# First two token tiles of x transposed by DMA instead of by identity matmuls, with the wq and wk loads issued from ACT's queue

## The chip, the cores and the metric

The kernel runs on one core of a Trainium2 chip. A core has TensorE (PE; its weight loads are listed as PEld), VectorE (DVE), ScalarE (ACT), GpSimd (POOL) and SyncE (SP), and 16 DMA engines that move data between the chip's memory and the core's on-chip memory. DMAs are issued here by SP, and a few by ACT, each through a hardware queue of its own. The metric is the device time of one execution in microseconds (us), as the median of several runs; lower is better.

## The reference

Two blocks read the same x (2048 tokens of 512) and a per-token gate mixes them. The heart of it:

```python
g = _sigmoid((x * gate_w).sum(-1, keepdims=True))
# A: linear attention, 32 heads of 16
q, k, v = split_heads(x @ wqkv)
pq, pk = phi(q), phi(k)             # phi(t) = where(t > 0, t + 1, exp(t)) + 1e-6
kv = einsum("bhsd,bhse->bhde", pk, v)
z = einsum("bhsd->bhd", pk)
o = einsum("bhqd,bhde->bhqe", pq, kv) / (einsum("bhqd,bhd->bhq", pq, z)[..., None] + 1e-6)
a = o @ wo
# B: gated MLP, inner width 1376
b = (_silu(x @ w1) * (x @ w3)) @ w2
return g * a + (1 - g) * b
```

All arrays are bfloat16.

## The kernel before

The 2048 tokens are 16 tiles of 128. A matmul of this chip contracts over the partitions, so x is needed in two forms: xN, with the tokens on the partitions (as it lies in memory), and xT, with the 512 features on the partitions in four k-chunks of 128.

The stages follow each other on TensorE, and the order of the instructions is written out by hand (`tc.manual_schedule()`): each engine runs its own list in program order and waits on semaphores where it needs another's result.

Stage 1, about the first 47 us, projects q and k for each tile with the weights wqk (512 rows by 1024 columns, four pieces of 128 rows, one for each k-chunk) and applies phi: ACT takes the exponential from PSUM (L182), DVE does the rest (L184, L187). `g_step` (L215) accumulates xN-transposed times phi(k) over all tiles in the banks 0 to 3 of PSUM; POOL sums phi(k) for z. Stage 2 runs, for each of four blocks of 512 tokens, the gated MLP's first half (`glu_step`, L259), and between its steps the small products that fold the attention into one matrix; then `out_step` (L423) makes each tile's output.

What concerns the change is the start:

- SP issues the loads in program order. The first is xN for the tokens 0 to 255 (L119). It lays two neighbouring tokens on each partition: partition p holds the tokens 2p and 2p+1, so "tile 0" is the even and "tile 1" the odd ones, and the output of these two tiles is written back in the same interleaved order (L451). Then come the four pieces of wqk (L116, `load_wqk`), then from L127 on the transposed loads of the tiles 2 to 15 (`load_xT`, L113, a DMA that transposes on the way) with the rest of xN between them (`natural`, L126), and then the weights of the later stages.
- ACT issues one small load, `touch` (L123): 16 columns of two k-chunks of wqkv into a tile that nothing reads.
- POOL builds a 128x128 identity matrix, `ident` (L69).
- TensorE starts with 13 matmuls on a constant (`warm_step`, L315, L331), whose result is not used. Then it transposes the tiles 0 and 1 itself: a matmul of a 128x128 block of xN with the identity (`transpose_block`, L321) puts the transposed block into PSUM, and DVE and ACT copy it into xT (L337 to L340, L352). Six of the eight blocks come first; the two of the last k-chunk come after the first four projection matmuls (L351).
- The first projections (`first_mm`, L344) go by k-chunk, as the pieces of wqk land: for the k-chunks 0 and 1 each of k and q for the tiles 0 and 1; then k alone for the chunks 2 and 3, and the two phi steps are started; then q for the chunks 2 and 3; then the k projection of tile 2 (L363). After the eight matmuls of chunk 0 and 1 the order is thus k tile 0, k tile 1 on piece 2, the same on piece 3, and ten more matmuls before the first `g_step` (L365).

The lines that set this order:

```python
for kc in range(2):
    for n, t in (("k", 0), ("q", 0), ("k", 1), ("q", 1)):
        first_mm(n, t, kc)
    ...
for kc in range(2, KC):
    for t in range(2):
        first_mm("k", t, kc)
```

Of the kernel before, what the change touches and what calls it, by code (L numbers as in the profile page):

```python
# [7 lines left out]

ACT = mybir.ActivationFunctionType
ALU = mybir.AluOpType  # L10
# [2 lines left out]
BF16 = mybir.dt.bfloat16  # L13
# [3 lines left out]
def kernel(  # L17
# [17 lines left out]
    nc = tc.nc  # L35
    P = nc.NUM_PARTITIONS

    Bb, S, D = A_x.shape
# [15 lines left out]
    x2d = A_x.flatten_outer_dims()  # L54
    out2d = out.flatten_outer_dims()
    x_t = x2d.rearrange("(t p) d -> p t d", p=P)
    wqkv_r = A_wqkv.rearrange("(kc d) n -> d kc n", d=P)
# [3 lines left out]
    consts = ctx.enter_context(tc.tile_pool(name="consts", bufs=1))  # L61
# [3 lines left out]
    ctx.enter_context(tc.manual_schedule())  # L65

    warm = nc.const_aps.tensor(1.0, [P, 256], BF16)
    ident = consts.tile([P, P], BF16, name="ident")
    make_identity(nc, ident[:])  # L69


    bmask = consts.tile([P, HPC, Dh], BF16, name="bmask")
# [2 lines left out]
        out=bmask[:], in_=bmask[:], pattern=[[-Dh, HPC], [0, Dh]], compare_op=ALU.is_ge,  # L75
# [3 lines left out]
        out=bmask[:], in_=bmask[:], pattern=[[Dh, HPC], [0, Dh]], compare_op=ALU.is_ge,  # L79
# [17 lines left out]
    xN = consts.tile([P, NT, D], BF16, name="xN")  # L97
    wqk = consts.tile([P, KC, 2 * D], BF16, name="wqk")
# [8 lines left out]
    xT = consts.tile([P, KC, S], BF16, name="xT")  # L107
    act_pre = consts.tile([P, 1], BF16, name="act_pre")
    dq = nc.sync

    def load_xT(t):
        ts = slice(t * P, (t + 1) * P)
        dq.dma_start(out=xT[:, :, ts], in_=x2d[ts, :], transpose=True)  # L113

    def load_wqk(kc):
        dq.dma_start(out=wqk[:, kc, :], in_=wqkv_r[:, kc, 0 : 2 * D])  # L116

    x_first = x2d[0 : 2 * P, :].rearrange("(p j) d -> p j d", j=2)
    dq.dma_start(out=xN[:, 0:2, :], in_=x_first)  # L119
    nc.scalar.activation(out=act_pre[:], in_=warm[:, 0:1], func=ACT.Exp)  # L120

    touch = consts.tile([P, 2, 16], BF16, name="touch")
    nc.scalar.dma_start(out=touch[:], in_=wqkv_r[:, 1:3, 0:16])  # L123
    for kc in range(KC):
        load_wqk(kc)
    natural = {3: (2, 4), 5: (4, 8), 8: (8, 16)}  # L126
    for t in range(2, NT):  # L127
        load_xT(t)
# [3 lines left out]
    with nc.allow_non_contiguous_dma(reason="gate column"):  # L132
        dq.dma_start(
            out=wr[:, :, 2 * FR : NR], in_=gate_w.rearrange("(kc d o) -> d kc o", d=P, o=1)
# [21 lines left out]
    bank = [psum.tile([P, D], FP32, name=f"bank{i}") for i in range(8)]  # L156
    turn = {"mm": 0, "ab": 0}

    def mm_tile():
        turn["mm"] += 1  # L160
        return bank[4 + (turn["mm"] - 1) % 4]

    def ab_tile():
        turn["ab"] += 1
        return bank[(turn["ab"] - 1) % 4]
# [149 lines left out]
    def warm_step(n):  # L315
        for _ in range(n):
            nc.tensor.matmul(  # L317
                bank[7][:, 0:256], lhsT=warm[:, 0:P], rhs=warm, start=True, stop=True
            )

    def transpose_block(t, kc, dst):  # L321

        nc.tensor.matmul(  # L323
            dst, lhsT=xN[:, t, kc * P : (kc + 1) * P], rhs=ident[:], start=True, stop=True
        )

    def transpose_kc(kc, ps):
        for t in range(2):
            transpose_block(t, kc, ps[:, t * P : (t + 1) * P])

    warm_step(13)  # L331

    for t in range(2):
        transpose_block(t, 0, bank[t][:, 0:P])
    transpose_kc(1, bank[2])
    transpose_kc(2, bank[3])
    nc.vector.tensor_copy(out=xT[:, 0, 0:P], in_=bank[0][:, 0:P])  # L337
    nc.scalar.activation(out=xT[:, 0, P : 2 * P], in_=bank[1][:, 0:P], func=ACT.Copy)
    nc.vector.tensor_copy(out=xT[:, 1, 0 : 2 * P], in_=bank[2][:, 0 : 2 * P])
    nc.scalar.activation(out=xT[:, 2, 0 : 2 * P], in_=bank[3][:, 0 : 2 * P], func=ACT.Copy)  # L340
    first = {(t, n): mm_tile() for n, t in (("k", 0), ("k", 1), ("q", 0), ("q", 1))}
    w_of = {"k": wk, "q": wq}

    def first_mm(n, t, kc):  # L344
        proj_mm(first[t, n], t, w_of[n], kc)

    for kc in range(2):
        for n, t in (("k", 0), ("q", 0), ("k", 1), ("q", 1)):
            first_mm(n, t, kc)
        if kc == 0:  # L350
            transpose_kc(3, bank[0])  # L351
            nc.vector.tensor_copy(out=xT[:, 3, 0 : 2 * P], in_=bank[0][:, 0 : 2 * P])  # L352
    for kc in range(2, KC):
        for t in range(2):
            first_mm("k", t, kc)
# [67 lines left out]
    def out_step(tb, tt):  # L423
        t = tb * TPB + tt
        ts = slice(t * P, (t + 1) * P)
        tl = slice(tt * P, (tt + 1) * P)
        a_ps = ab_tile()
        for c in range(KC):
            nc.tensor.matmul(  # L429
                a_ps[:], lhsT=pqT[:, c, ts], rhs=M2[:, c, :],  # L430
                start=(c == 0), stop=(c == KC - 1),
            )
        aga = work.tile([P, D], FP32, tag="aga", name="aga")
        nc.scalar.activation(out=aga[:], in_=a_ps[:], func=ACT.Copy, scale=g_all[:, t : t + 1])  # L434
        o = work.tile([P, D], BF16, tag="o", bufs=3, name="o")
        last = t == NT - 1
        for lo, w in ((0, 2 * P), (2 * P, P), (3 * P, P)) if last else ((0, D),):
            cs = slice(lo, lo + w)
            b_ps = ab_tile()
            for fc in range(FC + 1):  # L440
                n = P if fc < FC else FR
                nc.tensor.matmul(  # L442
                    b_ps[:, 0:w], lhsT=hT[tb][:n, fc, tl], rhs=w2[:n, fc, cs],
                    start=(fc == 0), stop=(fc == FC),
                )
            nc.vector.scalar_tensor_tensor(  # L446
                out=o[:, cs], in0=b_ps[:, 0:w], scalar=omg_all[:, t : t + 1], in1=aga[:, cs],
                op0=ALU.mult, op1=ALU.add,
            )
            if t < 2:  # L450
                rows = out2d[0 : 2 * P, :].rearrange("(p j) d -> p j d", j=2)[:, t, :]  # L451
            else:
                rows = out2d[ts, :]
            if last and w == P:

                if lo + w < D:
                    continue
                cs = slice(2 * P, D)
            dq.dma_start(out=rows[:, cs], in_=o[:, cs])
# [3 lines left out]
    for tb in range(NTB):  # L463
        for fc in range(FC):
            glu_step(tb, fc)
            if tb == 0:
                if fc in den_at:
                    den_step(den_at[fc])
                if fc == 2:
                    kv_step()  # L470
                if fc == 4:
                    m2_step()
                    z_order()
                    den_products(0)
                if fc == 7:
                    rem_step(0)
        for tt in range(TPB):
            out_step(tb, tt)
            if tb + 1 < NTB:
                if tt == 0:  # L480
                    hT[tb + 1] = work.tile([P, FC + 1, TB], BF16, tag="hT", name="hT")
                if tt == 1:
                    rem_step(tb + 1)
                den_step((tb + 1) * TPB + tt)
# [30 lines left out]
```

## Time and profile before

| What | Value |
|---|---|
| Time, median of 3 runs (lowest to highest) | 179.23 us (178.83 to 179.74) |
| Span of the profiled execution, first to last instruction | 177.9 us |
| TensorE busy | 174.3 us, 98% |
| DVE, ACT, POOL busy | 101.5, 62.2, 63.5 us |
| First DMA issue (SP, L119), first matmul (L317) | 0.81, 0.84 us |
| First transposing matmul (L323), first projection (L169) | 3.74, 4.51 us |
| First g_step matmul (L217) | 9.76 us |

For the profiled execution the page gives the span and no time of its own; the median of the runs lies 1.3 us above that span and the lowest run 0.9 us. TensorE's matmuls are pipelined: the profile's length of one matmul (0.38 us for 128x512) is longer than the distance from one to the next, so the pace is read from the chain, as the length of a piece divided by its count. "Landing" of a DMA is the time from its issue to the moment its completion is told.

### The profile page before, as it was taken

The numbers are of one execution on the slowest core, as the hardware profiler recorded it, in microseconds if no ns is written. First come the engines' busy times: TensorE is split into PE (matmuls) and PEld (weight loads), VectorE is DVE, ScalarE is ACT, GpSimd is POOL, SyncE is SP. The second block draws the span as 40 slices with busy tenths as digits, with TensorE's granted clock in tenths as the row PEclk, the third lists the DMA queues.
The fourth block names the chain that finished last, engine by engine and source line by source line (L and its number), as shares of the span: only waits on it lengthen the run. The fifth ranks groups of instructions, "written<-read, shape, count | busy, mean of one in ns | idle before, by whom it ended". The sixth has DMA issues, their size and how long they took to land.

```text
span 177.9 us, 2504 instructions
## 1 busy us (share of the span) xinstructions
PE 174.3 (98%) x879; PEld 84.1 (47%) x879; DVE 101.5 (57%) x195; ACT 62.2 (35%) x113; POOL 63.5 (36%) x105
## 2 busy tenths in 40 slices
PE   8999999999999999999999999999999999999993
PEld 5444444444454464644444464444445444444453
DVE  0299798888865888666344166634325564333222
ACT  3255444544744332331333223242321223342130
POOL 5077667557301676846300044540004432000000
DMA  6978959993103025243100013520000342000001
GB/s 175 266 209 233 168 100 315 391 350 111 33 0 29 0 55 66 66 95 106 29 0 4 0 33 85 94 57 4 0 0 29 88 92 59 0 0 0 29 33 59
DMA packets 29724, 15.41 MB, mean 87 GB/s; under 512 B 21552, under 2 KB 28048, under 8 KB 29712
## 3 DMA queue, kind: packets, MB, share of 16 engines
q1 hardware_dynamic: 29440, 15.25, 35.2%
q8 instruction: 7, 0.11, 0.3%
q10 hardware_dynamic: 272, 0.01, 0.1%
q14 instruction: 5, 0.04, 0.1%
HBM read 8.56 MB, written 2.10 MB: 60 GB/s over the span
## 4 chain that ended last, share of the span: by engine, by line
PE 98%; DVE 0%; issue 0%
PE bank L442 21%; PE bank L264 19%; PE bank L270 19%; PE bank L169 16%; PE bank L429 8%; PE bank L217 8%; PE bank L231 3%; PE bank L317 2%; PE bank L323 1%; PE bank L404 1%; PE bank L417 0%; DVE o L446 0%
## 5 line engine op out<-in xcount | busy, mean ns | idle before, releaser
L276 DVE TENSOR_TENSOR hT<-bank,sg 128x512 bf16<-128x512 f32 x40 | 27.3, 682 | 32.4 <-PE bank L270 32.4
L264 PE MATMUL bank<-xT,w 128*128 128x512 bf16 x160 | 41.1, 379 | 0.0
L270 PE MATMUL bank<-xT,w 128*128 128x512 bf16 x160 | 41.1, 379 | 0.0
L442 PE MATMUL bank<-w,hT 128*128 128x512 bf16 (+3 forms) x198 | 40.7, 355 | 0.0
L275 ACT ACTIVATE sg<-bank 128x512 bf16<-128x512 f32 x40 | 23.9, 597 | 46.7 <-PE bank L264 46.7
L298 POOL TENSOR_TENSOR pqs<-pq,rden 128x512 bf16<-128x512 bf16 x16 | 16.9, 1056 | 55.7 <-issue 48.2
L169 PE MATMUL bank<-wqk,xT 128*128 128x512 bf16 x128 | 31.2, 386 | 0.0
L442 PEld LDWEIGHTS <-hT 128*128 128x128 bf16 (+1 forms) x198 | 18.5, 98 | 19.8
L446 DVE SCALAR_TENSOR_TENSOR o<-bank,omg_all,aga 128x512 bf16<-128x512 f32 (+2 forms) x18 | 12.4, 692 | 25.6 <-PE bank L442 25.5
L201 POOL TENSOR_TENSOR zacc<-zacc,pk 128x128 f32<-128x128 f32 x56 | 23.3, 446 | 10.4 <-DVE pk L187 10.4
L270 PEld LDWEIGHTS <-w 128*128 128x128 bf16 x160 | 15.7, 98 | 18.9
L264 PEld LDWEIGHTS <-w 128*128 128x128 bf16 x160 | 15.6, 98 | 18.4
L434 ACT ACTIVATE aga<-bank,g_all 128x512 f32<-128x512 f32 x16 | 11.0, 688 | 28.9 <-PE bank L429 28.9
L169 PEld LDWEIGHTS <-xT 128*128 128x128 bf16 x128 | 12.6, 99 | 15.1 <-issue 0.6
L283 POOL TENSOR_TENSOR pr<-pq,zb 128x512 f32<-128x512 bf16 x16 | 18.5, 1156 | 0.1
L217 PE MATMUL bank<-pk,xN 128*128 128x512 bf16 x64 | 16.4, 379 | 0.0
L429 PE MATMUL bank<-M,pqT 128*128 128x512 bf16 x64 | 16.4, 378 | 0.0
L182 ACT ACTIVATE eq<-bank 128x512 bf16<-128x512 f32 x16 | 9.4, 598 | 16.0 <-PE bank L169 16.0
L187 DVE SCALAR_TENSOR_TENSOR pk<-bank,emk 128x512 bf16<-128x512 f32 x16 | 11.1, 692 | 1.6
L182 ACT ACTIVATE ek<-bank 128x512 bf16<-128x512 f32 x16 | 9.5, 597 | 7.1 <-PE bank L169 7.1
L187 DVE SCALAR_TENSOR_TENSOR pq<-bank,emq 128x512 bf16<-128x512 f32 x16 | 11.1, 692 | 0.5
L287 DVE TENSOR_REDUCE den<-pr 128x32 f32<-128x512 f32 x16 | 10.8, 676 | 0.0
(48 smaller groups left out, 82.6 us busy)
## 6 DMA issues: line engine op xcount, KB each, us to landing
w<-in_B_w_dram SPq DMA_DIRECT2D x3, 1280.0 KB, 10.1
out_dram<-o SPq DMA_DIRECT2D x15, 128.0 KB, 1.9
wqk<-in_A_wqkv_dram SPq DMA_DIRECT2D x4, 256.0 KB, 3.9
xN<-in_A_x_dram SPq DMA_DIRECT2D x1, 1024.0 KB, 5.8
xN<-in_A_x_dram SPq DMA_DIRECT2D x2, 256.0 KB, 3.1
xN<-in_A_x_dram SPq DMA_DIRECT2D x1, 512.0 KB, 3.7
wv<-in_A_wqkv_dram SPq DMA_DIRECT2D x1, 512.0 KB, 11.0
wo<-in_A_wo_dram SPq DMA_DIRECT2D x1, 512.0 KB, 12.0
```

Source lines behind the costliest of these rows:

```text
L169: nc.tensor.matmul(ps[:], lhsT=xT[:, kc, t * P : (t + 1) * P], rhs=w[:, kc, :], start=(kc == 0), stop=(kc == KC - 1),)
L182: nc.scalar.activation(out=e[:], in_=ps[:], func=ACT.Exp)
L187: nc.vector.scalar_tensor_tensor(out=dst, in0=ps[:], scalar=0.0, in1=em[:], op0=ALU.max, op1=ALU.add)
L201: nc.gpsimd.tensor_tensor(out=(zaccb if t == NT - 1 else zacc)[:, cs], in0=zacc[:, cs], in1=pk[t][:, cs], op=ALU.add,)
L217: nc.tensor.matmul(bank[kc][:], lhsT=xN[:, t, kc * P : (kc + 1) * P], rhs=pk[t][:], start=(t == 0), stop=(t == NT - 1),)
L264: nc.tensor.matmul(g_ps[:], lhsT=w1[:, kc, fs], rhs=xT[:, kc, tok], start=(kc == 0), stop=(kc == KC - 1),)
L270: nc.tensor.matmul(u_ps[:], lhsT=w3[:, kc, fs], rhs=xT[:, kc, tok], start=(kc == 0), stop=(kc == KC - 1),)
L275: nc.scalar.activation(out=sg[:], in_=g_ps[:], func=ACT.Silu)
L276: nc.vector.tensor_tensor(out=hT[tb][:, fc, :], in0=u_ps[:], in1=sg[:], op=ALU.mult)
L283: nc.gpsimd.tensor_tensor(out=pr[t][:], in0=pq[:, t, :], in1=zb[:], op=ALU.mult)
L429: nc.tensor.matmul(a_ps[:], lhsT=pqT[:, c, ts], rhs=M2[:, c, :], start=(c == 0), stop=(c == KC - 1),)
L442: nc.tensor.matmul(b_ps[:, 0:w], lhsT=hT[tb][:n, fc, tl], rhs=w2[:n, fc, cs], start=(fc == 0), stop=(fc == FC),)
```

## The change

The tiles 0 and 1 of x get their transposed form in the same way as the other tiles, by a transposing DMA. SP's first issue is the transposed load of tile 0, then that of tile 1, then xN for the two tiles, now in plain token order (partition p holds the tokens p and 128 + p). The four pieces of wqk are issued from ACT's queue. The identity matrix, the eight identity matmuls and the five copies out of PSUM are gone, as is `touch`. There are 14 matmuls on the constant at the start in place of 13. The output of the tiles 0 and 1 is written in plain order.

```diff
-    ident = consts.tile([P, P], BF16, name="ident")
-    make_identity(nc, ident[:])
...
     def load_wqk(kc):
-        dq.dma_start(out=wqk[:, kc, :], in_=wqkv_r[:, kc, 0 : 2 * D])
-
-    x_first = x2d[0 : 2 * P, :].rearrange("(p j) d -> p j d", j=2)
-    dq.dma_start(out=xN[:, 0:2, :], in_=x_first)
+        nc.scalar.dma_start(out=wqk[:, kc, :], in_=wqkv_r[:, kc, 0 : 2 * D])
+
+    load_xT(0)
     nc.scalar.activation(out=act_pre[:], in_=warm[:, 0:1], func=ACT.Exp)
-
-    touch = consts.tile([P, 2, 16], BF16, name="touch")
-    nc.scalar.dma_start(out=touch[:], in_=wqkv_r[:, 1:3, 0:16])
     for kc in range(KC):
         load_wqk(kc)
+    load_xT(1)
+    dq.dma_start(out=xN[:, 0:2, :], in_=x_t[:, 0:2, :])
...
-    warm_step(13)
-
-    for t in range(2):
-        transpose_block(t, 0, bank[t][:, 0:P])
-    transpose_kc(1, bank[2])
-    transpose_kc(2, bank[3])
-    nc.vector.tensor_copy(out=xT[:, 0, 0:P], in_=bank[0][:, 0:P])
-    nc.scalar.activation(out=xT[:, 0, P : 2 * P], in_=bank[1][:, 0:P], func=ACT.Copy)
-    nc.vector.tensor_copy(out=xT[:, 1, 0 : 2 * P], in_=bank[2][:, 0 : 2 * P])
-    nc.scalar.activation(out=xT[:, 2, 0 : 2 * P], in_=bank[3][:, 0 : 2 * P], func=ACT.Copy)
+    warm_step(14)
...
-        if kc == 0:
-            transpose_kc(3, bank[0])
-            nc.vector.tensor_copy(out=xT[:, 3, 0 : 2 * P], in_=bank[0][:, 0 : 2 * P])
...
-            if t < 2:
-                rows = out2d[0 : 2 * P, :].rearrange("(p j) d -> p j d", j=2)[:, t, :]
-            else:
-                rows = out2d[ts, :]
+            rows = out2d[ts, :]
```

More of the change, by code (lines that the diff above doesn't have):

```diff
@@ L6 @@
 from concourse._compat import with_exitstack
-from concourse.masks import make_identity
 ACT = mybir.ActivationFunctionType
@@ L319, in warm_step @@
             )
[L321 to L327, printed above, removed]
-        for t in range(2):
-            transpose_block(t, kc, ps[:, t * P : (t + 1) * P])
-    warm_step(13)
-    for t in range(2):
-        transpose_block(t, 0, bank[t][:, 0:P])
-    transpose_kc(1, bank[2])
-    transpose_kc(2, bank[3])
-    nc.vector.tensor_copy(out=xT[:, 0, 0:P], in_=bank[0][:, 0:P])
-    nc.scalar.activation(out=xT[:, 0, P : 2 * P], in_=bank[1][:, 0:P], func=ACT.Copy)
-    nc.vector.tensor_copy(out=xT[:, 1, 0 : 2 * P], in_=bank[2][:, 0 : 2 * P])
-    nc.scalar.activation(out=xT[:, 2, 0 : 2 * P], in_=bank[3][:, 0 : 2 * P], func=ACT.Copy)
+    warm_step(14)
     first = {(t, n): mm_tile() for n, t in (("k", 0), ("k", 1), ("q", 0), ("q", 1))}
```

## The prediction

> **What bounds the kernel now.** I read the page first: TensorE is busy for the whole span and is the whole chain that ended last.
>
> ```profile
> PE 174.3 (98%) x879; PEld 84.1 (47%) x879; DVE 101.5 (57%) x195; ACT 62.2 (35%) x113; POOL 63.5 (36%) x105
> ...
> PE 98%; DVE 0%; issue 0%
> ```
>
> So only what moves TensorE's chain counts, and the change touches that chain in its first 10 us alone. Next I read the chain in order of time for that stretch (start, length, piece):
>
> ```profile
> 0.84 2.93 PE bank L317 x13
> 3.77 0.79 PE bank L323 x6
> 4.56 1.79 PE bank L169 x4
> 6.36 0.11 PE bank L323 x2
> 6.47 3.45 PE bank L169 x16
> ```
>
> Two things are to be seen. There is no hole. And the same matmul (128x512, L169) costs 1.79/4 = 0.45 us before about 6.2 us and 3.45/16 = 0.216 us after it: TensorE runs at half pace until then, although the profile's granted clock reads 1.00 throughout. Then the issues in the timeline, and each one's time to landing in the DMA view (stretches that hold the issues of the first wqk piece, the last one, and the transposed tile 2):
>
> ```profile
> 0.81 0.40 SPq L119 DMA_DIRECT2D xN<-in_A_x_dram  x1
> 0.86 0.44 ACTq L123 DMA_DIRECT2D touch<-in_A_wqkv_dram  x1
> 1.27 1.83 SPq L116 DMA_DIRECT2D wqk<-in_A_wqkv_dram  x4
> 3.14 2.60 SPq L113 DMA_TRANSPOSE xT<-in_A_x_dram  x2
> ```
> ```profile
> wqk<-in_A_wqkv_dram SPq DMA_DIRECT2D x1, 256.0 KB, 3.2
> ...
> wqk<-in_A_wqkv_dram SPq DMA_DIRECT2D x1, 256.0 KB, 4.6
> ...
> xT<-in_A_x_dram SPq DMA_TRANSPOSE x1, 4.7
> ```
>
> The pieces of wqk thus land at 4.5, 5.1, 6.6 and 2.67 + 4.6 = 7.3 us. The last is needed by the seventh of the sixteen matmuls, which issues at 6.31 + 6 x 0.216 = 7.6: its cover is only 0.3 us. What the loads can reach, from the stages (last column GB/s):
>
> ```profile
> 1.75:2.50 0.75, 0.75 (x5) 0.49 (x4) 0.00 (x0) 0.54 (x2) 0.68 (x3) 1.00 0.81 115
> 2.50:4.50 2.00, 2.00 (x12) 1.24 (x11) 0.40 (x2) 0.28 (x1) 0.78 (x2) 1.00 1.09 351
> ```
>
> The DMA engines are full from 2.5 us on (share 1.09); nothing moves before 1.75 us.
>
> **The change part by part.** The sum is made against the profiled execution's span of 177.9 us; the median of the runs, 179.23, lies 1.3 above it, and I add the difference of spans to the median.
>
> *Work taken off TensorE:* eight identity matmuls. The first six run from 3.74 to 4.36, then TensorE waits for a copy until 4.51; the last two cost 0.14. That is 0.77 + 0.14 = 0.91 us. *Added:* one warm matmul, 0.21 (2.93/13). Net 0.70 us at the slow pace. But the pace steps up at a time, not after a count of work, so 0.7 us of slow work saved before 6.2 moves 0.7/0.427 = 1.6 matmuls into the slow part, which saves 1.6 x 0.211 = 0.35 us at the end. That is the most the removal can give.
>
> *Other engines:* DVE loses three copies (0.29, 0.42, 0.43) and ACT two (0.28, 0.39); beyond the waits counted above they lay beside TensorE. POOL loses the identity's two instructions (0.20 + 0.29); its next work that anyone waits for is at 9.73, so nothing. The ACT queue takes four issues of 0.44, from 0.86 to 2.6; ACT's next awaited activation is at 8.02, so nothing. The output of tiles 0 and 1 keeps its two 128 KB DMAs, in the middle of a stage that TensorE bounds: nothing.
>
> *SP's queue:* before, it issued xN (0.40) and four pieces (1.83), then tile 2 at 3.14. After: two transposes of 1.27 each (tile 0 at 0.81, tile 1 at 2.08), xN at 3.35, tile 2 at 3.95. Tile 2 and all behind it are issued 0.8 later. Tile 2, landed at 7.84, is needed at 8.90: 0.3 of cover remains. Tile 3 (4.48 + 3.8 = 8.3) is needed at 10.41, more. xN's first rows are needed at 9.76, issued 6.4 earlier. Without that cover, each costs its lateness one for one.
>
> *What TensorE now waits for:* two DMA transposes in place of the copies, and wqk from a second queue. A transposed store alone on the engines (pqT) takes 2.4 us to landing:
>
> ```profile
> GB/s 0 0 0 0 0 0 0 0 0 0 0 0 0 0 0 0 0 27 129 186 239 201 228 209 224 212 186 76 27 0 0 0 0 0 0 0 0 0 0 0
> ...
> pqT<-pqs SPq DMA_TRANSPOSE x2, 2.4
> ```
>
> Its 128 KB move at about 220 GB/s (0.6 us; a plain 256 KB piece takes 0.75 at 351), the first bytes 1.1 us after issue, and landing is told 0.5 to 0.6 after the last. How two queues divide the engines only the 8 KB touch shows (queues in 0 to 2.85 us, then in 2.85 to 3.35):
>
> ```profile
> q1 hardware_dynamic: 103, 0.21, 33.1%
> ```
> ```profile
> q1 hardware_dynamic: 95, 0.16, 85.1%
> q10 hardware_dynamic: 267, 0.01, 30.0%
> ```
>
> Both queues moved in the same half microsecond, at 340 GB/s together: a second queue adds no rate, it takes its share. The share for large transfers is not shown, so I bound it. If wqk goes first, in order of issue, its last piece lands at about 6.9. If SP's stream goes first and wqk gets the gaps, at about 10.8. I take equal bytes, since neither queue stood still beside the other:
>
> - 1.75 to 3.15: tile 0 and half of piece 0 (86 KB in the ramp, the rest 0.4 + 0.25 us). Tile 0 lands at 3.7.
> - to 4.1 (0.6 + 0.38): tile 1 and the other half. Both land at 4.7.
> - to 5.6 (2 x 0.75): xN's first 256 KB and piece 1, which lands at 6.2.
> - to 7.6 (2 x 0.98): tiles 2 and 3 and piece 2, which lands at 8.2.
> - to 9.1 (2 x 0.75): xN's next 256 KB and piece 3, which lands at 9.7.
>
> Before, the pieces had the engines to themselves once xN's first 256 KB was through. Now 0.9 MB of x is woven in with them. TensorE then starts at 4.7 (0.2 later than 4.51), and its first matmul of the fourth k-chunk issues at 9.7 in place of 7.6. Ten more issues follow at 0.216, as before; the phi chain behind them keeps its distance (pk of tile 0 ends 9.67 where TensorE wants it at 9.76, both shift alike). Sum: 9.7 - 7.6 = +2.1 us on the span; the 0.35 saved falls inside this wait. 179.2 + 2.1 = 181.3.
>
> The Trainium skill, "DMA: Bandwidth & Descriptors", section "Queues, rings and completion order", has each engine go round-robin between the queues, a packet of several descriptors at a time; the touch's 267 packets beside 95 of the other queue agree. By its section "Issuing engines are not separate DMA queues" a second issuer saves only issue time; the 340 GB/s above agree.
>
> **The rivals.**
>
> *The pace steps up later.* If wqk goes first, pieces land at about 4.1, 4.8, 5.6 and 6.9, but tile 1 queues behind three pieces and lands at 6.2. TensorE does two matmuls at 4.1 and stands until 6.2. Before, the step came after 5.4 us of unbroken work (0.84 to 6.2). If the holes put it off, eighteen matmuls follow at 0.427 until it comes. Bounds: no delay, 6.2 + 18 x 0.216 = 10.1 against 9.76, +0.3; a new 5.4 us from 6.2, 12.7 slow and 5.3 fast, 12.8, +3.0. Its middle is +1.7: 180.9. For it: holes of 0.4 to 2 us in the slow stretch. Against: no row of before has a hole. The Trainium skill, "TensorE: Matmul & The Clock Gate", Part 1, gives free-running windows of 3.4 us, of which one must be busy; by it the step would fall at about 9.6 and the time would be 181.3 (an estimate).
>
> *Hidden after all.* wqk goes first and the step stays at 6.2: +0.3 as just worked out, 179.5. For it: the touch, issued between xN and piece 0, moved only as xN's 128 rows ran out (103 by 2.85 us), like one line in order of issue. Against: ACT's table load ran until 2.08 and may have held the touch's start instead.
>
> *Not slower.* Tile 1 gets the idle engines' 2.45 us (2.08 + 2.45 = 4.5) and wqk, issued 0.41 earlier, lands by 6.9. TensorE starts at 4.1 and never stands. Then the 0.35 us come out: 178.9. It decides where tile 1 lands before 4.95 and piece 3 before 7.3. Against: both on full engines at once need more bytes than 351 GB/s moves by then.
>
> **How the numbers follow.** Shares of the engines make wqk late (forecast): 0.42, own range 180.4 to 182.4 (SP first: 10.8 - 7.6 = 3.2). Late step: 0.25. Hidden: 0.20. Not slower: 0.13. Half a per cent, 0.9 us, is about what a measurement of this kernel can tell from no change. Forecast and late step are nearly all slower by more, 0.65 of 0.67. The third and most of the fourth are within it, 0.30; faster than 178.3 needs an earlier step too, 0.05. The range: 179.0 leaves about 0.1 below, 182.5 about 0.1 above (late step and late wqk together).
>
> **What would show it.** In the profile after: TensorE idle before L169, released by the wqk DMA, 1 to 2 us in all between 6 and 10 us; the pieces of wqk landing near 3.8, 4.9, 6.5 and 7.5 us after their issue; SP's tile 0 landing near 3.7. From 12 us on every piece of the chain shifted alike. A matmul pace of 0.427 beyond 6.5 us speaks for the late step; wqk landed by 7.3 and tile 1 at 6 for issue order. The prediction is wrong if wqk's last piece lands before 8 us, or if a hole opens behind 12 us.

## The result and the profile after

The changed kernel takes 184.59 us (median of four runs, 182.87 to 185.5) against 179.16 us for the kernel before in the same job: 1.0286 times as long, with a 95% interval of 1.0228 to 1.0343. A second job with the same kernel gave 183.87 us and 1.0234 (1.0196 to 1.0271). The change makes the kernel 2.3 to 2.9% slower.

The profiled execution is the quickest of its four, 182.87 us with a span of 181.2. The page, busy times and the engines of the chain that ended last:

```profile
PE 175.0 (97%) x872; PEld 83.7 (46%) x872; DVE 99.6 (55%) x192; ACT 61.5 (34%) x111; POOL 62.7 (35%) x103
...
PE 92%; DMA 5%; DVE 1%; issue 0%; ACTq 0%; DVEq 0%
```

TensorE's chain was 98% of the span before. Now 5% of it are DMAs. The chain in order of time shows where (start, length, piece):

```profile
0.81 4.81 DMA xT<-in_A_x_dram
5.62 0.02 issue
5.64 0.34 ACTq L113
5.97 0.04 issue
6.01 4.25 DMA wqk<-in_A_wqkv_dram
10.26 0.04 issue
10.30 2.32 PE bank L164 x10
```

These seven lines name the wait. The end of the first projections hangs on the last piece of wqk, which landed at 10.26 after an issue at 6.01; that issue came just after another on ACT's queue at 5.64; and that one came 0.02 us after the transposed tile 0 had landed. A load waited to be *issued* until a different load had *landed*. (The ten matmuls of the last line are the two k projections on piece 3 and eight more before the first `g_step`; the description of the kernel before says ten more.) The timeline of the same execution has both queues and TensorE:

```profile
0.81 2.60 SPq L110 DMA_TRANSPOSE xT<-in_A_x_dram  x2
0.86 0.88 ACTq L113 DMA_DIRECT2D wqk<-in_A_wqkv_dram  x2
...
5.64 1.03 ACTq L113 DMA_DIRECT2D wqk<-in_A_wqkv_dram  x2
5.67 3.60 PE L164 MATMUL bank<-wqk,xT 128*128 128x512 bf16 x8 [1.68 <-DMA xT<-in_A_x_dram]
9.46 0.60 PE L164 MATMUL bank<-wqk,xT 128*128 128x512 bf16 x2 [0.20 <-DMA wqk<-in_A_wqkv_dram]
10.30 2.32 PE L164 MATMUL bank<-wqk,xT 128*128 128x512 bf16 x10 [0.24 <-DMA wqk<-in_A_wqkv_dram]
```

Three things are to be seen. ACT's queue issues two pieces at once and then nothing for almost four microseconds. Tile 0 lands at 5.62, 4.8 us after its issue, so TensorE, done with the constant matmuls at 4.0, stands for 1.68 us. And the eight matmuls after the hole run at about 0.43 us each, the last ten at 0.22: the pace, which stepped up near 6.2 us before, now steps up between 9.05 and 9.5. The profile books only 0.44 us as waits for wqk, because the eight slow matmuls fill most of the time in which the pieces were missing anyway.

The first `g_step` matmul, the mark behind the first projections, is at 12.46 us instead of 9.76: 2.70 of the 3.24 us of longer span. Of the rest, 0.26 comes at 53 us, where DVE waits 1.07 us for a transposing DMA (0.23 before) and TensorE then for DVE:

```profile
52.83 0.69 DVE L357 TENSOR_REDUCE zTb<-zaT 128x4 bf16<-128x512 bf16 x1 [1.07 <-DMA zaT<-zaccb]
```

That DMA's issue took 2.33 us here and 1.19 before. In a second profile of the same kernel (the first run below) the chain passes that stage through TensorE alone, and loses 0.18 us there. The last 0.27 lies behind the last DVE instruction, and I did not follow it.

### The profile page after: what moved, and what is told of

The parts are those of the page before. It is cut to its first block, busy times and chain, and to the rows that moved or that the text cites. A ratio compares the mean times of both kernels' runs of the same rounds, so it can differ in the third digit from the quotient of the medians.

```text
span 181.2 us, 2484 instructions
## 1 busy us (share of the span) xinstructions
PE 175.0 (97%) x872; PEld 83.7 (46%) x872; DVE 99.6 (55%) x192; ACT 61.5 (34%) x111; POOL 62.7 (35%) x103
## 4 chain that ended last, share of the span: by engine, by line
PE 92%; DMA 5%; DVE 1%; issue 0%; ACTq 0%; DVEq 0%
PE bank L416 21%; PE bank L265 19%; PE bank L259 19%; PE bank L164 14%; PE bank L403 8%; PE bank L212 8%; PE bank L226 3%; DMA xT<-in_A_x_dram 3%; DMA wqk<-in_A_wqkv_dram 2%; PE bank L378 0%; PE bank L391 0%; DVE hT L271 0%; DVE o L420 0%; ACTq L113 0%; DVEq L271 0%
## 5 line engine op out<-in xcount | busy, mean ns | idle before, releaser
L164 PE MATMUL bank<-wqk,xT 128*128 128x512 bf16 x128 | 32.3, 395 | 2.1 <-DMA xT<-in_A_x_dram 1.7
L196 POOL TENSOR_TENSOR zacc<-zacc,pk 128x128 f32<-128x128 f32 x56 | 23.1, 442 | 10.4 <-DVE pk L182 9.0
L177 ACT ACTIVATE ek<-bank 128x512 bf16<-128x512 f32 x16 | 9.4, 597 | 12.5 <-PE bank L164 12.2
L179 DVE TENSOR_SCALAR emk<-ek 128x512 bf16<-128x512 bf16 x16 | 6.9, 430 | 11.3 <-ACT ek L177 11.3
L182 DVE SCALAR_TENSOR_TENSOR pk<-bank,emk 128x512 bf16<-128x512 f32 x16 | 11.1, 691 | 2.0 <-PE bank L164 0.5
L182 DVE SCALAR_TENSOR_TENSOR pq<-bank,emq 128x512 bf16<-128x512 f32 x16 | 11.1, 692 | 0.6
## 6 DMA issues: line engine op xcount, KB each, us to landing
wv<-in_A_wqkv_dram SPq DMA_DIRECT2D x1, 512.0 KB, 11.1
```

Of the source, the lines that this page charges most:

```text
L164: nc.tensor.matmul(ps[:], lhsT=xT[:, kc, t * P : (t + 1) * P], rhs=w[:, kc, :], start=(kc == 0), stop=(kc == KC - 1),)
L177: nc.scalar.activation(out=e[:], in_=ps[:], func=ACT.Exp)
L182: nc.vector.scalar_tensor_tensor(out=dst, in0=ps[:], scalar=0.0, in1=em[:], op0=ALU.max, op1=ALU.add)
L196: nc.gpsimd.tensor_tensor(out=(zaccb if t == NT - 1 else zacc)[:, cs], in0=zacc[:, cs], in1=pk[t][:, cs], op=ALU.add,)
```

## The experiments

Three theories stood. W, a wait: pieces of wqk are held back at ACT's queue until tile 0 has landed. P, the pace: the hole in TensorE's early work puts off the step. S, from my prediction: the two queues share the engines and the loads of x push wqk back.

The program's own list of ACT's instructions after the change supports W. Each DMA signals its landing on one of eight completion semaphores, which are handed out in turn over both queues; a ninth DMA must first wait for the landing of the one that had its semaphore. The order is not that of the source lines: tile 0, tile 1, xN, piece 0, tiles 2 and 3, piece 1, xN for the tiles 2 and 3, and then, as the ninth, piece 2. The list, with what each load waits for:

```
 3 L113 DMACopy wqk<-in_A_wqkv_dram 128x1024 x2
 4 L113 DMACopy wqk<-in_A_wqkv_dram 128x1024 [waits DMAHW0_49]
 5 L113 DMACopy wqk<-in_A_wqkv_dram 128x1024 [waits DMAHW3_49]
```

Semaphore 0 is that of tile 0, semaphore 3 that of piece 0. In the kernel before, all four pieces were among the first eight DMAs, and the ninth was xN for the tiles 2 and 3, which nobody needed soon.

**The changed kernel again.** No edit.

> The changed kernel once more, unaltered, to see how much of its start differs from one execution to the next: its profiled execution took 182.9 us, its timed runs up to 185.5. Theory W (a wait): in the profile, pieces 2 and 3 of wqk are issued on ACT's queue only at 5.64 and 6.01 us, right after the transposed tile 0 landed at 5.62, and land at 9.4 and 10.3. The issue waits for that landing; it should do so again, wherever tile 0 lands. Theory P (pace): TensorE stands from 3.8 to 5.7 us and its matmuls keep the slow pace of 0.427 us until about 9.5 instead of 6.2; in slower runs the step should come later still, up to 13 us, and the time should follow it: 1.7 us more for a step 3.4 us later. If the spread comes from neither, tile 0's landing must differ.

Measured: 183.87 us (183.33 to 186.67), span of the profiled execution 181.5.

```profile
4.97 1.04 ACTq L113 DMA_DIRECT2D wqk<-in_A_wqkv_dram  x2
5.00 3.59 PE L164 MATMUL bank<-wqk,xT 128*128 128x512 bf16 x8 [1.01 <-DMA xT<-in_A_x_dram]
...
10.73 2.32 PE L164 MATMUL bank<-wqk,xT 128*128 128x512 bf16 x10 [0.97 <-DMA wqk<-in_A_wqkv_dram]
```

Tile 0 landed at 4.96 this time, and piece 2 was issued at 4.97: the issue follows the landing, as W says. The last piece still came no sooner (10.69, 5.3 us after its issue).

**wqk in two loads.**

```diff
-    def load_wqk(kc):
-        nc.scalar.dma_start(out=wqk[:, kc, :], in_=wqkv_r[:, kc, 0 : 2 * D])
+    def load_wqk(k0, k1):
+        nc.scalar.dma_start(out=wqk[:, k0:k1, :], in_=wqkv_r[:, k0:k1, 0 : 2 * D])
...
-    for kc in range(KC):
-        load_wqk(kc)
+    for k0 in range(0, KC, 2):
+        load_wqk(k0, k0 + 2)
```

> wqk in two DMAs of two k-chunks (512 KB each) on ACT's queue instead of four of 256 KB, nothing else changed. Theory W: only two loads are issued there, neither waits, both are issued by 1.8 us and the second lands before 7 us instead of 10.3; the first projections are then held by tile 0 (5.6) and the slow pace alone: eight or nine matmuls at 0.427 to 9.5, the other eleven or twelve at 0.216, first g_step at about 12.0 instead of 12.46, span 180.4 to 180.9. My recorded theory S (the two queues share the engines, and the x loads push wqk back): the second half of wqk lands after 9 us all the same and the span stays at 181 or above.

Measured: 183.43 us (182.95 to 184.35), span 182.0. The loads did what W says: both were issued by 1.8 us and had landed by 6.5. S's claim that wqk comes after 9 us anyway falls. But the gain did not come, because tile 0 landed later still, at 6.87 us. The chain:

```profile
0.81 6.07 DMA xT<-in_A_x_dram
6.87 0.05 issue
6.92 7.00 PE bank L164 x20
```

TensorE's hole grew to 2.93 us, and twelve of the twenty matmuls then ran at 0.427, until about 12.0. So the engines are shared indeed, but the side that loses is the transposing load, not wqk.

**More constant matmuls.**

```diff
-    warm_step(14)
+    warm_step(24)
```

> 24 matmuls on the constant in place of 14, which fills TensorE from 0.84 to 5.9 us; the loads are untouched. Theory P: without the hole the pace steps up near 6.2 to 6.5 us as in the kernel before; the first eight projections run at 0.216, then TensorE waits for pieces 2 and 3, which land at 9.4 and 10.3 as before, so the profiled span stays near 181 (within 0.4), but the timed runs lose their slow tail: median 182.5 to 183.2, spread under 1 us. Theory W alone (the pace is of no account): spread and median as in the changed kernel, 184.6.

Measured: 183.01 us (182.71 to 184.54), span 181.0.

```profile
5.92 2.22 PE L164 MATMUL bank<-wqk,xT 128*128 128x512 bf16 x8
8.51 0.59 PE L164 MATMUL bank<-wqk,xT 128*128 128x512 bf16 x2 [0.37 <-DMA wqk<-in_A_wqkv_dram]
10.41 2.32 PE L164 MATMUL bank<-wqk,xT 128*128 128x512 bf16 x10 [1.31 <-DMA wqk<-in_A_wqkv_dram]
```

No hole ahead of the projections, and the step came at about 6.6. The span hardly moved, as the last piece (10.37) bounds it, and the median fell by 0.9 to 1.6 us against the two jobs with the hole. One of four runs still took 184.5, so the spread is smaller, not gone.

**All loads on SP's queue.**

```diff
-        nc.scalar.dma_start(out=wqk[:, kc, :], in_=wqkv_r[:, kc, 0 : 2 * D])
+        dq.dma_start(out=wqk[:, kc, :], in_=wqkv_r[:, kc, 0 : 2 * D])
...
     load_xT(0)
+    load_xT(1)
     nc.scalar.activation(out=act_pre[:], in_=warm[:, 0:1], func=ACT.Exp)
     for kc in range(KC):
         load_wqk(kc)
-    load_xT(1)
```

> The changed kernel with all loads on SP's queue: tile 0, tile 1, the four pieces of wqk, then xN. ACT issues nothing. Theory S: tile 0, with no plain load beside it, lands near 3.4 us (2.5 after issue) instead of 5.6, tile 1 near 4.7; the pieces, issued from 3.4 on, land between 5.7 and 8.2, none waits for a landing. First projection at 5.8; the hole of 2 us keeps the slow pace until 9.5 (theory P), so the first g_step comes at 11.9 to 12.1, span 180.6. If tile 0 lands after 5 us here too, its lateness is not from the second queue.

Measured: 182.76 us (182.39 to 184.17), span 182.5. Tile 0's line in the DMA view (last column: us from issue to landing), first of the changed kernel, then of this one:

```profile
xT<-in_A_x_dram SPq DMA_TRANSPOSE x1, 4.8
```
```profile
xT<-in_A_x_dram SPq DMA_TRANSPOSE x1, 2.5
```

The same transposing load, issued at the same moment, takes 2.5 to 2.7 us in the three runs in which ACT issues no load, and 4.1 to 6.1 us beside plain loads from ACT's queue. That settles what makes tile 0 late. The kernel gains almost nothing, since wqk starts 2.6 us later: the pieces landed at 6.4, 7.1, 9.3 and 9.9, and a hole of 2.47 us put the step off to 12.5, against the 9.5 that I expected.

**Two loads and no hole.** The two-load edit with `warm_step(30)`.

> wqk in two loads on ACT's queue (nothing waits for a landing to be issued) and 30 matmuls on the constant, which keep TensorE busy until 7.2 us. Both suspected costs are taken away, the late landing of tile 0 (6.9 us with two loads) stays. Theories W and P together: the pace steps up near 6.2 to 6.5; all twenty first projections run at 0.216 from about 7.2, so the first g_step comes at 7.2 + 20 x 0.216 = 11.5 against 9.76 in the kernel before, span 179.7, time 181.0 to 181.4. Compared with 24 constant matmuls and four loads (first g_step 12.57) the wait on the landings is worth 1.1 us. If a third cost is hidden in the loads, the g_step stays at 12 or later.

Measured: 181.29 us (181.18 to 181.35), 1.0103 (1.0076 to 1.013) of the kernel before; span 179.5.

```profile
6.95 4.27 PE L164 MATMUL bank<-wqk,xT 128*128 128x512 bf16 x19
11.27 0.81 PE L212 MATMUL bank<-pk,xN 128*128 128x512 bf16 x3
```

As W and P together predict (span 179.7), and the spread of the runs, 1.4 us with the hole, is down to 0.2.

**The kernel before with a hole.** `warm_step(5)` in place of 13 in the kernel before, nothing else.

> The kernel before with 5 matmuls on the constant in place of 13: TensorE stands from 1.9 to 3.74 us, a hole of 1.7 us as in the changed kernel, and every load is as before. Theory P: the hole alone puts the step off to about 9.5; from 4.5 on, matmuls at 0.427 until then, so the first g_step comes 1.5 to 1.8 us later (11.3 to 11.6), span 179.5, time about 180.9. If holes don't matter, the time is that of the kernel before.

Measured: 180.31 us (179.87 to 180.81), 1.0047 (1.0021 to 1.0074); span 178.5.

```profile
3.70 0.82 PE L323 MATMUL bank<-ident,xN 128*128 128x128 bf16 x6 [1.63 <-DMA xN<-in_A_x_dram]
...
6.35 4.13 PE L169 MATMUL bank<-wqk,xT 128*128 128x512 bf16 x16
```

The loads are untouched and the kernel is slower, so a hole alone costs time. But only 0.56 us at the first `g_step` (10.32), a third of what I expected: the step came at 7.4, not 9.5. That is 3.7 us after the hole's end.

**The kernel before with wqk on ACT's queue.** The identity matmuls stay; `dq` becomes `nc.scalar` in `load_wqk`.

> The kernel before with its identity matmuls, and only the four loads of wqk moved to ACT's queue. Theory W: the third piece on ACT's queue must wait for the landing of an earlier load whose completion semaphore it takes over (the small touch or piece 0, landed by about 4 to 5 us) and lands after 8 us; TensorE waits for it 1 to 2 us at the pace of 0.216; span 178.9 to 179.9. Theory P: no hole before 6.2, so the step stays near 6.2. If the queue does not matter, the span is 177.9.

Measured: 184.8 us (184.3 to 185.66), 1.0304 (1.0262 to 1.0347); span 182.6. As slow as the whole change, and by far more than I expected. The timeline shows what I had overlooked:

```profile
6.36 0.84 ACTq L116 DMA_DIRECT2D wqk<-in_A_wqkv_dram  x2
7.25 0.28 ACT L338 ACTIVATE xT<-bank 128x128 bf16<-128x128 f32 x1 [4.95 <-DMA xT<-in_A_x_dram]
...
7.58 1.03 PE L169 MATMUL bank<-wqk,xT 128*128 128x512 bf16 x2 [1.89 <-ACT xT L338]
```

The third piece on ACT's queue waits for a transposed tile (landed at 6.34, issue at 6.36), and ACT works in program order: its copy of the transposed block stands behind the waiting issue, from 4.2 to 7.25 us, and TensorE waits for that copy. In the change itself nothing urgent stands behind the loads on ACT, which is why there the wait shows only in wqk.

**The kernel before without the unused load.** `touch` and its DMA left out.

> The kernel before without the small load that nothing reads. Both theories: nothing changes but which load a later one must wait for; time within 0.5 us of the kernel before.

Measured: 179.6 us, 1.0011 (0.9994 to 1.0028). This part of the change is worth nothing. In its profile the pace stepped up at 4.3 us already, and TensorE then waited 0.32 us for piece 1; the first `g_step` came at 9.34.

**No wait for piece 2.** One line moved, in the kernel with 24 constant matmuls:

```diff
-    nc.scalar.activation(out=act_pre[:], in_=warm[:, 0:1], func=ACT.Exp)
     for kc in range(KC):
         load_wqk(kc)
+    nc.scalar.activation(out=act_pre[:], in_=warm[:, 0:1], func=ACT.Exp)
```

> The kernel with 24 constant matmuls and four loads of wqk on ACT's queue, with one line moved: the dummy exponential on ACT comes after the four loads instead of ahead of them. The loads then stand earlier in the order in which completion semaphores are handed out: piece 2 gets a fresh one and waits for nothing; only piece 3 still waits, for the landing of tile 0. Theory W: piece 2 is issued near 1.8 us instead of 5.03 and lands by 6.5 instead of 8.5; piece 3 is issued right after tile 0 lands and lands after 8, earlier than 10.4 as nothing of piece 2 is ahead of it; first g_step at 10.6 to 12.2 instead of 12.57, span 179 to 180.6. If the landing times come from shared engines alone, they stay at 8.5 and 10.4 and the span at 181.

Measured: 180.83 us (180.76 to 181.82), 1.0086 (1.0056 to 1.0116); span 179.1.

```profile
0.80 3.07 ACTq L113 DMA_DIRECT2D wqk<-in_A_wqkv_dram  x4
...
5.58 0.61 PE L164 MATMUL bank<-wqk,xT 128*128 128x512 bf16 x2 [0.47 <-DMA xT<-in_A_x_dram]
6.75 4.06 PE L164 MATMUL bank<-wqk,xT 128*128 128x512 bf16 x18 [0.57 <-DMA xT<-in_A_x_dram]
10.64 0.59 PE L212 MATMUL bank<-pk,xN 128*128 128x512 bf16 x2
```

All four pieces were out by 3.87 us and landed by 8.2. In one detail I was wrong: with the new order, piece 3 takes the semaphore of piece 0 (landed at 3.48, issue at 3.50), not that of tile 0. Against the run with 24 constant matmuls the wait is worth 1.93 us at the first `g_step` (12.57 to 10.64) and 2.2 us of time. This is the direct proof of W: the loads, the queue and the bytes are the same, and the order in which semaphores are handed out differs (the exponential itself comes later too, but nothing in the chain waits for it). What TensorE now waits for is tile 1, landed at 6.70; it stands twice, for 0.47 and 0.57 us, and the pace stays.

**All on SP without the hole.** The single-queue kernel with `warm_step(27)`.

> All loads on SP's queue (tile 0, tile 1, four pieces of wqk, xN) as run before, with 27 constant matmuls, so that TensorE has no hole up to 6.6 us. The loads should land as they did: pieces at 6.4, 7.1, 9.3 and 9.9. Theory P: the pace steps up before 6.6 instead of at 12.5, and what is left is the fourth piece: first g_step at 9.95 + 2.16 = 12.1 instead of 13.3, span 180.3 to 180.6. If the late step costs nothing there, the span stays at 182.5.

Measured: 182.25 us (181.56 to 182.61), span 179.9, first `g_step` at 11.60. The pieces landed at 6.4, 7.2, 8.8 and 9.4, a little earlier than before, and the fourth bounds the end:

```profile
6.46 1.89 PE L164 MATMUL bank<-wqk,xT 128*128 128x512 bf16 x8 [0.77 <-DMA wqk<-in_A_wqkv_dram]
8.80 2.97 PE L164 MATMUL bank<-wqk,xT 128*128 128x512 bf16 x12 [0.45 <-DMA wqk<-in_A_wqkv_dram]
```

The mark comes 2.1 us sooner between these two profiles (13.74 to 11.60); about 0.5 of it is the earlier landing of the fourth piece, which leaves about 1.6 for the late step. The median moved by only 0.5: the profile with the hole, at 184.17 us, was the slowest of its four runs, so the hole does not cost this much every time.

**One queue, tile 1 behind wqk.** The changed kernel with `dq` in `load_wqk` (so: tile 0, four pieces, tile 1, xN, all on SP) and `warm_step(22)`.

> All loads on SP's queue in the order tile 0, four pieces of wqk, tile 1, xN; 22 constant matmuls (TensorE busy to 5.5 us). It asks what the transposed loads cost when no queue and no semaphore is in the way. Tile 0 lands at 3.4; the pieces, issued from 2.1 to 3.9, land from 5.2 to 8; tile 1, behind them in one queue, lands at 8 to 8.7 as tile 2 did behind the pieces in the kernel before (7.8). TensorE does two matmuls near 5.6 and then stands until tile 1 is there; eighteen matmuls at 0.216 follow: first g_step at 12.0 to 12.7, span 180.1 to 180.9. If it comes near 10, the order in the queue was all that the change got wrong.

Measured: 184.34 us (183.93 to 184.37), span 182.5, first `g_step` at 14.28, two microseconds later than I expected. Tile 0 landed at 3.4, the last piece at 8.1, tile 1 at 8.66, all as expected. What I had not expected is in the timeline and in the stages (PEclk is the third figure from the end):

```profile
8.70 5.75 PE L164 MATMUL bank<-wqk,xT 128*128 128x512 bf16 x18 [2.46 <-DMA xT<-in_A_x_dram]
```
```profile
5.00:8.70 3.70, 1.25 (x6) 0.44 (x4) 0.00 (x0) 0.00 (x0) 0.00 (x0) 1.00 1.12 264
...
9.40:12.70 3.30, 3.30 (x9) 1.22 (x8) 0.00 (x0) 0.40 (x1) 0.00 (x0) 0.51 0.77 185
```

After the hole three matmuls ran at 0.22, and then the granted clock fell to 0.51 for 3.3 us, at 0.427 a matmul. A hole of 2.46 us does not only delay the step up: some half a microsecond after its end the pace was taken back. The trace's own record of the clock gives the edges (PE's busy time is the second figure behind the stretch):

```profile
5.81:9.22 3.41, 0.95 (x5) 0.29 (x4) 0.00 (x0) 0.00 (x0) 0.00 (x0) 1.00 1.16 249
9.22:12.63 3.41, 3.41 (x10) 1.24 (x9) 0.00 (x0) 0.33 (x1) 0.00 (x0) 0.50 0.81 193
```

The pace fell at the end of a stretch of 3.41 us in which TensorE was busy for 0.95, and it stayed low for another 3.41 us.

**The hole without the wait.** The moved line, with the 14 constant matmuls of the change.

> The changed kernel with its 14 constant matmuls, and only the dummy exponential moved behind the four loads on ACT's queue, so that no load there waits for tile 0. It is the fourth corner of a square: wait and hole (183.9 to 184.6 us), wait without hole (183.0), neither (180.8), and here the hole without the wait. Loads as in the run with 24 constant matmuls: tile 0 at 5.5, tile 1 at 6.7, the last piece at 8.2. Theory P: the hole from 3.8 to 5.6 keeps the slow pace to somewhere between 9.0 and 12.4; then the first g_step comes at 11.8 to 13.3 instead of 10.6, and the time is 182.0 to 183.6: with the wait gone the hole costs more than the 0.9 to 1.6 us that it costs beside the wait, since nothing covers it. If wait and hole simply add, the time is 181.7 to 182.4.

Measured: 182.88 us (180.75 to 183.11), span 181.0, first `g_step` at 12.51.

```profile
6.95 5.73 PE L164 MATMUL bank<-wqk,xT 128*128 128x512 bf16 x18 [1.12 <-DMA xT<-in_A_x_dram]
```
```profile
7.00:11.00 4.00, 4.00 (x11) 1.44 (x12) 0.00 (x0) 0.23 (x1) 0.00 (x0) 0.58 1.05 262
```

The two matmuls before 7 us ran at the full pace already, and it fell back after holes of 1.39 and 1.12 us, to return at 10.4. So the late step that I expected is not what this profile shows: its step up came at 3.5 us, ahead of the hole, and was taken back. One of the four runs took 180.75, as quick as without the hole; the other two took 183.1 with a mean granted clock of 1.00, so they cannot have fallen back in this way, and their traces were not taken. The square of medians (us):

| | holes of 1 to 1.7 us | no early hole over 0.6 us |
|---|---|---|
| pieces wait for a landing | 184.59, 183.87 | 183.01 |
| no such wait | 182.88 | 180.83 |

The wait is worth 1.0 to 2.2 us and the hole 0.9 to 2.1, each most when the other is gone. The corners are not alike in all else: the lower left one has two holes, 2.51 us together, and medians of four or five runs with spreads of 1.1 to 3.3 us stand behind the figures. What is left in the last corner, 1.2 to 1.3 us against the kernel before (179.5 to 179.6 in these jobs), lies mostly with the transposed tiles: 0.88 us of it is there at the first `g_step` (10.64 against 9.76), and the chain ahead of that hangs on tile 1, which landed at 6.7 beside wqk, against 4.6 to 4.8 with no load on ACT's queue.

## Why the prediction was right or wrong

The direction was right and the size was not: 181.3 us forecast, 184.59 measured, outside the range that ended at 182.5.

*What held.* Only TensorE's chain in the first 10 us mattered, and from 13 us on all shifts alike but for 0.26 and the 0.27 at the end. The removal of the identity matmuls gave nothing at the end. The last piece, not TensorE's work, bounds the first projections: it landed at 10.26 and 10.69 where I had 9.7. Leaving out `touch` was worth nothing by itself (1.0011); the identity on POOL and the output order were not tried apart, and neither is in the chain after.

*The step that failed* is "The ACT queue takes four issues of 0.44, from 0.86 to 2.6". Two were issued there; the third went out at 5.64 and 4.97, when tile 0 had landed. I priced the move to another queue by the issue time alone and did not ask which landing each issue must wait for, although the program shows it. Counted from their own issue the pieces were quick: 2.7, 3.5, 3.8 and 4.2 us to landing, where I had 3.8, 4.9, 6.5 and 7.5; the lateness was in the issue. So the forecast's lateness of wqk was nearly right for a wrong reason: equal shares would have made the pieces late by crowding, and with all four issued early beside the same loads of x the last one landed at 8.2, not 9.7.

*Equal shares* failed with it. Of the two streams it was the transposing one that lost: tile 0 landed at 5.62 and 4.96 where I had 3.7, and piece 0 at 3.60 and piece 1 at 4.77 where I had 4.7 and 6.2. Between my bounds, the first two pieces lay near "wqk goes first". With no wait for piece 2 the last two landed at 6.23 and 8.20, between that bound (5.6 and 6.9) and equal shares (8.2 and 9.7).

*The late step* I had as a rival to the forecast, with 0.25, when both came at once: wqk late and TensorE standing. Its hole of 1.68 us was within the 0.4 to 2 us given there. Apart, either gives about 183, as the square's side corners show; together they give 184 to 184.6. I had put that case into the 0.1 above the range. The corners add up where my sum had one term of 2.1 us: from the kernel before, 1.2 to 1.3 us for the transposed tiles, 2.2 for the wait, and 0.9 to 1.6 for the hole beside it.

*Its size:* the rule of the Trainium skill, "TensorE: Matmul & The Clock Gate", Part 1, put the step at about 9.6 (the prediction's estimate), and the profile has it between 9.05 and 9.5. Counting 5.4 us anew from the end of the hole, the upper bound from the rows, would have given 11.1. Over all profiles here the step up came 2.7 to 6.0 us after TensorE last began to work without a hole of 1 us or more (at 3.5 and 3.9 after a start at 0.84 in the two runs with the moved line, 7.4 after 3.70, 12.0 after 6.92, 12.5 after 6.46), so that it came near 9.6 in this profile is in part luck. The trace's record of the clock, which begins with the step up, fits that rule's free-running windows of 3.4 us: where the pace fell back, the full and the half stretch were 3.41 us each (5.81 to 9.22 to 12.63, and 3.53 to 6.95 to 10.36). Counting such stretches back from the thirteen recorded steps up, TensorE was busy for 2.69 us or more in the one just before, and for 2.61 or less in the one before that. It was busy for 0.95 and 0.91 us in the two stretches after which the pace fell, and for 2.15 or more in those behind a step up after which it stayed. So the busy share of such a stretch decided here, not the length of one hole, and where the stretches begin differs from execution to execution. That is read out of the profiles and not tried by an edit.

*Not settled:* the three other runs of the first job took up to 2.6 us more than the profiled one. Two of them have a mean granted clock of 0.991, the figure of the two profiled executions in which the pace fell back for 3.41 us. That makes the same cause likely; their traces were not taken, so it is argued, not shown. Nor is it shown why a transposing load loses against plain ones on the other queue, only that it does. Two figures of the prediction are a little off without consequence: 2.93/13 is 0.225 and not 0.21 (the starts are 0.21 apart), and the loads of x in its list come to 1.0 MB, not 0.9.

## What to carry to other kernels

A DMA moved to another queue still draws from the same eight completion semaphores as the loads of the other queue, and may draw later than before: list, for each early load, the landing that its issue must wait for, and what stands behind it on that engine; here one moved line of code was worth 2.2 us. At the start of a kernel, a hole of one to three microseconds in TensorE's work costs time beyond the wait itself, because the pace then steps up late or falls back: filling it with constant matmuls, with the loads issued as they were, won 0.8 to 2.1 us in four pairs of runs here and 0.5 in a fifth. So cover it, and price late data and late pace together, not as alternatives. And a transposing load is quick only by itself: beside a stream of plain loads, transposing the first tiles on an idle TensorE was cheaper.

## What the hardware showed that I had not expected

- A transposing load of 128 KB landed 2.5 to 2.7 us after issue with no load on the other queue and 4.1 to 6.1 us after it beside plain loads from the other queue, with the longest delay beside the largest loads (512 KB each).
- TensorE's granted clock fell to half for 3.41 us after a hole of 2.46 us, and again after holes of 1.39 and 1.12 us, where it had already been at the full pace; both times TensorE had been busy for under 1 us of the 3.41 before. The Trainium skill, "TensorE: Matmul & The Clock Gate", in its table of what matters for kernels, warns of gaps above about 3 us; here shorter ones were enough, and the measurement decides.
- The slow stretch at the start of every kernel does not show in the granted clock, which reads 1.00 while a matmul takes 0.427 us instead of 0.216; the fall back does show. In the trace the record of the clock begins only with the step up.
